# Windowed attention with sinks, then a gated feed-forward, on one core: k and q of seven tiles in packets of 4 tokens, tiles of the batches by turns, the first mask by TensorE, priorities by kind of work

## The chip, the cores and the metric

The kernel runs on one core of a Trainium2 chip. The metric is the device time of one execution in microseconds (us). The time of before is the median of three runs. Every duration of a single instruction comes from one further execution that the hardware profiler recorded.

## The reference

Inputs are q, k and v of shape (4, 8, 768, 64) in float32: 4 batches, 8 heads, 768 positions, head width 64. The number of sinks is 4 and the window is 128. Output is (3072, 512) in float32.

```python
scores = q @ k.T / sqrt(64)
keep = (key < 4) | ((0 <= query - key) & (query - key < 128))
a = softmax(where(keep, scores, -1e9))
x = (a @ v)                      # heads side by side: 3072 tokens x 512
xn = x / sqrt(mean(x*x) + 1e-6) * rms_g
g, val = xn @ w_gate, xn @ w_val # 512 x 1536 each
out = (g * sigmoid(g) * val) @ w_out   # 1536 x 512
```

## The kernel before

**Tiles and visits.** The 3072 tokens are 24 tiles of 128 tokens, six for each batch, taken batch after batch (`bt = b * NT + t`). A tile is attended to in two visits of four heads each, so there are 48 visits. A tile needs its own block of keys and the block before it in the same batch, and the four sink keys. The first block of a batch (`t == 0`) has only its own block.

**A tile's way in.** Three transfers issued by SyncE (SP) bring k, q and v of a tile as `[128 tokens, 8 heads, 64]` in float32 (`load`, L415): each run of memory is one head of one token, 256 bytes. `casts` (L317, L323) turns them into bf16. `qk_unit` transposes k and q, for the first 12 tiles by TensorE (L471) and a copy out of PSUM (L315, L317), later by a DMA transpose. The products with the sink keys are made there too (L491).

**A visit** (`visit`): score products into PSUM (L545). In a first block VectorE writes -1e30 over the forbidden half of the scores with a predicated copy (L558). In every other block it copies the older block's scores into the forbidden half (L567), so that one softmax row of 128 columns holds exactly the window, and copies the sink scores in (L578). Then a row maximum (L587), four exponents on ScalarE (L591), the exponent of the sinks (L597, L601), a transpose of the probabilities (TensorE for the first 12 visits, L609, then DMA, L618), two selections on GpSimd that split the current block from the older one (L625, L629), the products with v (L638, L646, L651), and a division by the row sum (L662, L665).

**After two visits** `rows` makes the normalisation (L675 to L685) and a transpose into `xnt` (L696, or DMA, L688).

**The feed-forward.** The first four tiles and the last two are groups of one tile, the others of two. `f_unit` makes one unit: gate products (L721), tanh on ScalarE (L735), value products (L721), two VectorE products (L739, L742) into `h`. A tile has three units, a pair of tiles six. `o_unit` makes the output product of a tile (L753), a copy (L764) and a store (L767). The weights come as nine transfers issued by GpSimd, which cast to bf16 on the way (L441, L447). `FIRST` gives their order and the earliest time of each in the plan; the first of them really waits until k of the second tile has landed (`HOLD`).

**The order of the work** is made by a planner. Every operation has engines with estimated times, what it reads and writes, and a rank. The planner plays the time forward and always picks the operation that can start first, and among equal starts the lowest rank. PSUM has one pair of banks for scores and six single banks (two singles also serve as a pair for the first 20 visits). The order that comes out is fixed on each engine. `ROOM` adds a margin, after 70 us of the plan, to the end of an operation of another engine that TensorE or VectorE waits for. `LEAD` lets visits run ahead of the feed-forward: visit n waits for feed-forward piece 2 * (n - LEAD). `fill` puts matmuls on a blank tile (L819) where the plan leaves TensorE free before 38 us.

Of the kernel before, what the change touches and what calls it, by code (L numbers as in the profile page):

```python
# [9 lines left out]
ALU = mybir.AluOpType  # L10
# [6 lines left out]
P = 128  # L17
NEG = -1.0e30
AHEAD = 2
LEAD = 12  # L20
NL = 3
# [6 lines left out]
FFRANK = 1000.0  # L28
QK_DMA = 12
FIRST = "g0:2 v0:10 g1:13 v1:18 g2:20 v2:27 o1:38 o2:39 o0:39"  # L30
SHARES = {"SP": 0.2, "POOL": 0.95}
ROOM = {"PE": 0.6, "DVE": 0.2}
ROOM_FROM = 70.0
# [4 lines left out]
SPLIT = 20  # L38
PACE = 7
# [19 lines left out]
class Plan:  # L59
# [10 lines left out]
    def op(self, alts, fn, reads=(), writes=(), rank=0.0, takes=None, banks=(), after=()):  # L70
        o = Op(alts, fn, rank)
# [18 lines left out]
    def dma(self, queue, issue, moves, fn, reads=(), writes=(), rank=0.0, lag=1.1, after=()):  # L90

        o = self.op([(queue, issue, issue)], fn, reads=reads, rank=rank, after=after)
        m = Op(queue, None, rank)
        m.moves, m.begin, m.left, m.lag = None, 0.0, moves, lag
        m.waits.add(o)
        for w in writes:
            if w in self.wrote:
                o.waits.add(self.wrote[w])
            o.waits.update(self.read.pop(w, ()))
            self.wrote[w] = m  # L100
        for r in reads:
            self.read[r].append(m)
        o.waits.discard(o)
        o.moves = m
        self.ops.append(m)
        return o

    def order(self):
# [59 lines left out]
        while len(done) < len(self.ops):  # L168
            pick = None
            for o in ready:  # L170
# [9 lines left out]
                key = (s, o.rank)  # L180
                if pick is None or key < pick[0]:
                    pick = (key, o, c, a)
            t = event()
            if t is not None and (pick is None or t <= pick[0][0]):
# [49 lines left out]
def kernel(  # L234
# [93 lines left out]
    KQT = ring("KQT", 2, [P, NT, 2, HP, P], BF16)  # L328
    KT = [x[:, :, 0] for x in KQT]
    QT = [x[:, :, 1] for x in KQT]  # L330
    KS = ring("KS", 2, [P, HP, 2, NS], BF16)
    VS = ring("VS", 2, [P, 2, 4 * VW], BF16)
# [8 lines left out]
    negbig = const.tile([P, 1], FP32, name="negbig")  # L341
    m_old = const.tile([P, P], I16, name="m_old")
    m_first = const.tile([P, P], I16, name="m_first")
# [33 lines left out]
    def c_masks():  # L377

        for m in (m_old, m_first):
            nc.gpsimd.memset(m, 1)  # L380
            nc.gpsimd.affine_select(
                out=m, in_=m, compare_op=ALU.is_gt, fill=0,
                base=0, pattern=[[1, P]], channel_multiplier=-1,
            )
        nc.gpsimd.memset(m_first[:, 0:NS], 0)

    def c_small():
        nc.vector.memset(negbig, NEG)
        nc.vector.memset(nhalf, -0.5)
        for i in range(2):  # L390
# [4 lines left out]
    def c_sinks():  # L395
        for i in range(2):
# [3 lines left out]

    plan.op(on(POOL=0.8), c_ident, writes=["ident"], rank=-3000)
    plan.op(on(DVE=0.6), c_small, writes=["small", ("KS", 0), ("KS", 1)] + [("V", i) for i in range(10)], rank=-3000)
    plan.op(on(ACT=1.4), lambda: nc.scalar.activation(out=warm, in_=nhalf, func=ACT.Exp), reads=["small"], rank=-3000)
    plan.op(on(POOL=1.4), c_masks, writes=["masks"], rank=-2999)
    plan.op(on(DVE=1.2), c_sinks, writes=[("VS", 0), ("VS", 1)] + [("PK", i) for i in range(NPS)], rank=-2999)

# [3 lines left out]
    def load(bt, rank):  # L410

        b, t = divmod(bt, NT)
        for i, src in enumerate((k, q, v)):
            n = (3 * bt + i) % len(ST)
            LOADED[bt, i] = plan.dma("SP", 0.45, 1.33, lambda src=src, n=n: nc.sync.dma_start(  # L415
                out=ST[n], in_=src[b, :, t * P:(t + 1) * P, :].rearrange("h t d -> t h d"),
            ), writes=[("ST", n)], rank=rank + 0.1 * i,
                after=VISIT[2 * bt - PACE:2 * bt - PACE + 1] if 2 * bt >= PACE else [])

    def casts(bt, rank):  # L420

        for i, nm in enumerate("kqv"):
            n = (3 * bt + i) % len(ST)
            if nm == "v":
                dst, key = V16[bt % len(V16)][:, :, 0:D], ("V", bt % len(V16))
            else:
                m = bt % len(SO)
                dst, key = SO[m][:, i].rearrange("p (h d) -> p h d", d=D), ("SO", m, i)
            if nm == "q":
                alts = on(DVE=0.4, ACT=on_act(DM))  # L430
                fn = lambda e, dst=dst, n=n: times(e, dst, ST[n], scale)
            else:
                alts = cast(DM) if bt < NT else on(POOL=0.13 + 0.84e-3 * DM)
                fn = lambda e, dst=dst, n=n: copy(e, dst, ST[n])
            plan.op(alts, fn, reads=[("ST", n)], writes=[key], rank=rank + 0.1 * i)

    def load_w(nm, i, rank):
# [3 lines left out]
        return plan.dma("POOL", 0.78, 3.1 if c1 - c0 > 256 else 1.8, lag=1.5, fn=lambda: nc.gpsimd.dma_start(  # L441
# [3 lines left out]
    def load_wo(part, rank):  # L445
        f0, f1 = 4 * part, 4 * part + 4
        return plan.dma("POOL", 0.78, 3.1, lag=1.5, fn=lambda: nc.gpsimd.dma_start(  # L447
# [5 lines left out]
    def qk_unit(b, t, rank):  # L453

        par = b % 2
        bt = b * NT + t
# [3 lines left out]
        if bt >= QK_DMA:  # L460
            plan.dma("SP", 1.2, 1.6, lambda: nc.sync.dma_start_transpose(
                out=KQT[par][:, t].rearrange("c a h p -> c (a h) p"), in_=SO[m].rearrange("p a d -> p (a d)")),
                reads=[("SO", m, 0), ("SO", m, 1)], writes=[("k", par, t), ("q", par, t)], rank=rank)
        else:
            for i, nm in enumerate("kq"):
                bk = Banks(ONES)

                def tr(i=i, bk=bk):
                    pt = bank(bk).bitcast(BF16)
                    for hp in range(HP):  # L470
                        nc.tensor.transpose(  # L471
                            out=pt[:, hp * P:(hp + 1) * P], in_=SO[m][:, i, hp * P:(hp + 1) * P], identity=ident,
                        )

                o = plan.op(on(PE=0.23), tr, reads=["ident", ("SO", m, i)], takes=bk, rank=rank + 0.1 * i, after=after)
                plan.op(evac(HP * P), lambda e, bk=bk, i=i: copy(
# [405 lines left out]
```

## Time and profile before

| | |
|---|---|
| median of three runs | 267.3 us (266.77 to 267.5) |
| the profiled execution's own time | 267.78 us |
| its span, first to last instruction | 266.0 us |
| granted TensorE clock | 0.999 |
| HBM read, written | 28.57 MB, 6.29 MB |
| transfers of k, q, v | 24 each of 256 KB, 4.6, 4.9, 5.1 us to landing (median) |
| weight transfers | 9 of 512 KB, medians of 9.2 to 10.6 us to landing |
| first gate product, first output product | at 19.56 us, at 55.86 us |

PE is TensorE's matmuls, PEld its loads of stationary weights, DVE is VectorE, ACT ScalarE, POOL GpSimd, SP SyncE. A group line gives line, engine, operation, output and input, count, then busy time and mean nanoseconds of one, then the engine's idle time before it and what ended that. In a chain line the numbers are start, duration and what. Matmuls overlap in a pipeline, so the durations of their records add up to more than the time that they hold the engine.

### The profile page before, as it was taken

What the parts mean: (1) busy time and instruction counts of PE and PEld (TensorE: products, weight loads), DVE (VectorE), ACT (ScalarE), POOL (GpSimd) and SP (SyncE); (2) the same over time, 40 slices, a digit from 0 to 9 for tenths busy, and PEclk for the clock granted to TensorE, in tenths of its full rate; (3) what the DMA queues carried; (4) which work ended last, traced back from release to release, by engine and by line L of the source; (5) the groups of instructions that cost most, each with busy time, mean ns of one, the idle gap of its engine ahead of it and who ended that gap; (6) DMA issues with size and microseconds to landing.
All of it is one profiled execution on the core that took longest, in us unless ns stands there. A gap on an engine that the chain in (4) does not pass through costs nothing.

```text
span 266.0 us, 7200 instructions
## 1 busy us (share of the span) xinstructions
PE 254.8 (96%) x2685; PEld 190.1 (71%) x2702; DVE 211.0 (79%) x510; ACT 147.3 (55%) x419; POOL 140.0 (53%) x272
## 2 busy tenths in 40 slices
PE   8998998999998999999999999999999999999994
PEld 6686877865666857858758668587587686785981
DVE  3977699999989898988959959679689599494641
ACT  2463676867767647456645467356664555551430
POOL 3566646579446897563637645734534446243100
PEclk9999999999999999999999999999999999999999
DMA  8999999979999989999999969969792431412311
GB/s 162 214 182 210 209 209 199 204 157 233 209 170 165 199 170 187 163 246 192 216 148 240 172 119 226 173 165 179 158 195 40 92 86 25 123 28 46 101 42 39
DMA packets 129155, 41.83 MB, mean 157 GB/s; under 512 B 121312, under 2 KB 125920, under 8 KB 129120
## 3 DMA queue, kind: packets, MB, share of 16 engines
q1 hardware_dynamic: 124368, 36.65, 75.2%
q0 software_dynamic: 4752, 4.72, 10.9%
q8 instruction: 21, 0.34, 0.6%
q14 instruction: 14, 0.11, 0.1%
HBM read 28.57 MB, written 6.29 MB: 131 GB/s over the span
## 4 chain that ended last, share of the span: by engine, by line
PE 81%; DVE 10%; DMA 5%; issue 2%; ACT 1%; POOL 0%; POOLq 0%
PE one L721 45%; PE one L753 22%; DMA wg_bf<-in_moe_w_gate_dram 5%; PE pair L545 4%; PE one L819 3%; DVE nmax L587 3%; PE one L646 2%; PE one L651 2%; PE one L638 1%; PE one L471 1%; DVE one L567 1%; PE one L609 1%; DVE h L742 1%; DVE so L323 1%; DVE x L665 1%
## 5 line engine op out<-in xcount | busy, mean ns | idle before, releaser
L721 PE MATMUL one<-xnt,wg_bf 128*128 128x256 bf16 (+1 forms) x720 | 72.0, 251 | 1.7 <-DMA wg_bf<-in_moe_w_gate_dram 1.0
L721 PE MATMUL one<-xnt,wv_bf 128*128 128x256 bf16 (+1 forms) x720 | 72.2, 251 | 0.3 <-DMA wv_bf<-in_moe_w_val_dram 0.2
L753 PE MATMUL one<-wo_bf,h 128*128 128x512 bf16 x271 | 68.1, 379 | 0.9
L735 ACT ACTIVATE th<-one 128x512 bf16<-128x512 f32 x72 | 42.7, 602 | 42.3 <-PE one L721 35.0
L721 PEld LDWEIGHTS <-wg_bf 128*128 128x128 bf16 x720 | 57.4, 98 | 10.5 <-issue 2.0
L721 PEld LDWEIGHTS <-wv_bf 128*128 128x128 bf16 x720 | 57.3, 98 | 9.7 <-issue 3.2
L739 DVE SCALAR_TENSOR_TENSOR p<-th,one 128x512 bf16<-128x512 bf16 x72 | 48.3, 677 | 15.1 <-ACT th L735 14.8
L591 ACT ACTIVATE ps<-pair,nmax 128x128 bf16<-128x128 f32 x152 | 43.7, 370 | 16.5 <-DVE nmax L587 8.6
L742 DVE TENSOR_TENSOR h<-p,one 128x512 bf16<-128x512 bf16 x72 | 48.3, 679 | 3.3 <-PE one L721 2.1
L753 PEld LDWEIGHTS <-h 128*128 128x128 bf16 x288 | 25.7, 98 | 26.3 <-issue 2.5
L683 POOL TENSOR_TENSOR xg<-x,grow 128x512 bf16<-128x512 bf16 x24 | 27.9, 1165 | 29.5 <-DVE x L665 27.1
L625 POOL TENSOR_SCALAR_AFFINE_SELECT cur<-pt 128x512 bf16<-128x512 bf16 x40 | 25.6, 639 | 29.5 <-DMA pt<-ps 21.5
L764 ACT ACTIVATE osb<-one 128x512 f32<-128x512 f32 x24 | 14.4, 599 | 24.0 <-PE one L753 23.8
L587 DVE TENSOR_REDUCE nmax<-pair 128x4 f32<-128x528 f32 (+1 forms) x38 | 26.5, 696 | 0.5
L567 DVE COPY_PREDICATED pair<-m_old,pair 128x512 f32<-128x512 int16 x32 | 22.0, 688 | 5.0 <-PE pair L545 4.0
L629 POOL TENSOR_SCALAR_AFFINE_SELECT old<-pt 128x512 bf16<-128x512 bf16 x40 | 25.8, 644 | 0.1
L597 POOL TENSOR_TENSOR sd<-sk,nmax 128x16 f32<-128x16 f32 x40 | 8.9, 224 | 25.7 <-DVE nmax L587 23.3
L665 DVE TENSOR_TENSOR x<-one,rden 128x256 bf16<-128x256 f32 x48 | 20.0, 417 | 0.5
L675 ACT ACTIVATE sq<-x 128x512 bf16<-128x512 bf16 x24 | 15.2, 634 | 9.2 <-DVE x L665 7.2
L819 PE MATMUL one<-blank 128*128 128x256 bf16 x132 | 19.2, 295 | 1.2 <-POOL blank L370 1.2
L662 DVE RECIPROCAL rden<-one 128x4 f32<-128x4 f32 x48 | 8.4, 176 | 10.8 <-PE one L651 9.4
L819 PEld LDWEIGHTS <-blank 128*128 128x128 bf16 x132 | 13.4, 106 | 3.8 <-POOL blank L370 1.2
(73 smaller groups left out, 305.2 us busy)
## 6 DMA issues: line engine op xcount, KB each, us to landing
st<-in_k_dram SPq DMA_DIRECT2D x24, 256.0 KB, 4.6
st<-in_q_dram SPq DMA_DIRECT2D x24, 256.0 KB, 4.9
st<-in_v_dram SPq DMA_DIRECT2D x24, 256.0 KB, 5.1
out_dram<-osb SPq DMA_DIRECT2D x24, 256.0 KB, 2.9
wg_bf<-in_moe_w_gate_dram POOLq DMA_DIRECT2D x3, 512.0 KB, 10.5
wv_bf<-in_moe_w_val_dram POOLq DMA_DIRECT2D x3, 512.0 KB, 9.2
wo_bf<-in_moe_w_out_dram POOLq DMA_DIRECT2D x3, 512.0 KB, 10.6
pt<-ps SPq DMA_TRANSPOSE x36, 3.3
```

What stands on the lines that cost most here:

```text
L567: nc.vector.copy_predicated(out=ap[:, :, P:2 * P], mask=m_old.unsqueeze(1).to_broadcast((P, hs.stop - hs.start, P)), data=ap[:, :, 0:P],)
L587: nc.vector.tensor_reduce(out=nm[:, hs], in_=ap[:, :, c0:2 * P], axis=AX.X, op=ALU.max, negate=True)
L591: plan.op(on(ACT=0.253), lambda h=h: nc.scalar.activation(out=PSM[r3][:, h, :], in_=head(h)[:, P:2 * P], func=ACT.Exp, bias=nm[:, h:h + 1] ...
L625: plan.op(on(POOL=0.6), lambda: nc.gpsimd.affine_select(out=cur, in_=PTT[r3][:, 0:4, :], compare_op=ALU.is_ge, fill=0.0, base=0, pattern=[ ...
L629: plan.op(on(POOL=0.6), lambda: nc.gpsimd.affine_select(out=old, in_=PTT[r3][:, 0:4, :], compare_op=ALU.is_gt, fill=0.0, base=0, pattern=[ ...
L683: plan.op(on(POOL=1.05), lambda: nc.gpsimd.tensor_tensor(out=xg, in0=X16[r], in1=grow, op=ALU.mult), reads=xs + ["g"], writes=[("XG", bt % ...
L721: nc.tensor.matmul(out=bank(bk)[:, i * n * P:(i + 1) * n * P].rearrange("p (t c) -> p t c", c=P), lhsT=w[:, kt, ft * P:(ft + 1) * P], rhs= ...
L735: plan.op(on(ACT=0.49), lambda: nc.scalar.activation(out=th, in_=b3(gb), func=ACT.Tanh, scale=0.5), banks=[gb], after=[o], writes=[("TH", ...
L739: plan.op(on(DVE=0.6), lambda: nc.vector.scalar_tensor_tensor(out=p1, in0=th, scalar=1.0, in1=b3(gb), op0=ALU.add, op1=ALU.mult,), banks=[ ...
L742: plan.op(on(DVE=0.6), lambda: nc.vector.tensor_tensor(out=HT[g % len(HT)][:, f0:f1, 0:n * P], in0=p1, in1=b3(vb), op=ALU.mult,), banks=[v ...
L753: nc.tensor.matmul(out=bank(bk)[:, 0:DM], lhsT=h[:, ft, tb * P:(tb + 1) * P], rhs=wo_bf[:, ft, :], start=(ft == 0), stop=(ft == FTN - 1),)
L819: done = plan.fill(done, lambda: nc.tensor.matmul(out=ONE[-1][:, 0:256], lhsT=blank[:, 0:P], rhs=blank, start=True, stop=True), 0.109)
```

## The change

1. **Packets.** k and q of the first seven tiles come with 4 tokens of one head in a packet (1 KB) and each in two transfers, one for every second head. Partitions then hold (head pair, group of four tokens), the casts reorder within the row, TensorE transposes as before, and the copy out of PSUM (`put`) writes with a stride of four to restore the order of tokens.
2. **Tiles by turns.** `bt = t * B + b`: the first four tiles are the first blocks of the four batches, then the second blocks, and so on. The k and q store keeps two blocks for each batch, used alternately, so "own" and "older" half of the scores swap places from block to block. Sink tables exist for all four batches.
3. **First mask.** In a first block TensorE writes the mask into PSUM (identity times a mask tile) and the score product is accumulated on it; VectorE's predicated copy goes.
4. **Plan.** Ranks are shifted by kind of operation, SP may take a lower rank within 0.4 us, and LEAD, the number of tiles in flight, the margins, the pace of the loads and the order and earliest times of the weights have new values.

```diff
-LEAD = 12
-NL = 3
+LEAD = 10
+NL = 4
+WIDE = 7
-FIRST = "g0:2 v0:10 g1:13 v1:18 g2:20 v2:27 o1:38 o2:39 o0:39"
+FIRST = "g0:10@2 g1:16@5 v1:15@6 v0:22@8 g2:19@0 v2:26@1 o0:33@7 o1:33@3 o2:30@4"
-ROOM = {"PE": 0.6, "DVE": 0.2}
-ROOM_FROM = 70.0
+ROOM = {"PE": 0.1, "DVE": 0.3, "ACT": 0.05, "POOL": 0.4, "SP": 0.05}
+WINDOW = {"SP": 0.4}
+WINDOW_TO = 100
+SHIFT = {"exp_sinks": 20, "load_2": 5, ... "square": 40, "greatest": -29.5, ... "exp": -1}
+EARLY = {"kq": 16, "av": -14.5, "m2": 16, ... "exp_sinks": -6.5}
+FEED = {"gate": 1000, "tanh": 6, "val": 10, "p1": 6, "h": 10, "out": 1000, "out_copy": 10, "store": 9}
+BEGIN = {(3, 2): 11, (5, 2): 36, (7, 0): 31, (8, 0): 38, (8, 1): 45, (9, 2): 79}
+ROOM_FROM = 50.0
+SOON = 6
+PACE0 = 9
...
+    def place(self, kind, rank):
+        if rank < -900:
+            return rank
+        if kind in FEED:
+            return (rank - FFRANK) / 2 + FEED[kind]
+        return rank + SHIFT.get(kind, 0.0) + (EARLY.get(kind, 0.0) if rank < 16 else 0.0)
...
+                until = s + (WINDOW.get(e, 0.0) if s < WINDOW_TO else 0.0)
+                for c in can:
+                    if c[3][0] == e and c[0][0] <= until and c[0][1] < pick[0][1] - 1e-9:
+                        pick = c
...
-    KQT = ring("KQT", 2, [P, NT, 2, HP, P], BF16)
+    KQT = ring("KQT", B, [P, 2, 2, HP, P], BF16)
...
-        b, t = divmod(bt, NT)
+        t, b = divmod(bt, B)
+        pace = PACE if bt >= SOON else PACE0
...
+            for half in (range(2) if bt < WIDE and i < 2 else (None,)):
+                wide = half is not None
+                LOADED[bt, i] = plan.dma(
+                    f"load_{i}", "SP", 0.45, 0.4 if wide else 1.2, ... nc.sync.dma_start(
+                        out=ST[n].rearrange("p (r j) d -> p r (j d)", r=2)[:, half] if wide else ST[n],
+                        in_=src[b].rearrange("(g r) t d -> r g t d", r=2)[half, :, t * P:(t + 1) * P].rearrange(
+                            "g (a j) d -> g a (j d)", j=4)
+                        if wide else src[b, :, t * P:(t + 1) * P, :].rearrange("h t d -> t h d"),
...
+                if bt < WIDE:
+                    dst, src = (x.rearrange(f"p ({y}) d -> p r j d", r=2) for x, y in ((dst, "j r"), (src, "r j")))
...
+                    if wide:
+                        copy(e, KQT[par][:, sl, i].rearrange("c g (a j) -> c j g a", j=4),
+                             pt.rearrange("c (j g a) -> c j g a", j=4, g=HP))
...
+        def m_mm():
+            for hs, ap in parts():
+                for i in range(0, hs.stop - hs.start, 2):
+                    nc.tensor.matmul(
+                        out=ap[:, i:i + 2, 0:P], lhsT=ident, rhs=m_first.unsqueeze(1).to_broadcast((P, 2, P)),
+                        start=True, stop=False, skip_group_check=True,
+                    )
+        if t == 0:
+            first = plan.op("mask_mm", on(PE=0.22), m_mm, takes=sb, reads=["ident", "first"], ...)
...
-        if t == 0:
-            def mask():
-                for hs, ap in parts():
-                    nc.vector.copy_predicated(
-                        out=ap[:, :, P:2 * P], mask=m_first.unsqueeze(1).to_broadcast((P, w, P)),
-                        data=negbig.unsqueeze(2).to_broadcast((P, w, P)),
-                    )
...
-    for b in range(B):
-        for t in range(NT):
-            bt = b * NT + t
+    for t in range(NT):
+        for b in range(B):
+            bt = t * B + b
             casts(bt, 2.0 * bt - AHEAD)
-            load_tile(bt + NL)
             qk_unit(b, t, 2.0 * bt - AHEAD)
...
+            load_tile(bt + NL)
             rows(bt, float(vn))
```

## The prediction

> **What bounds the kernel now.** I read the busy shares first, then the same table cut into stretches, then the DMA queues of the first 40 us, the chain of waits, and the cost groups of the lines that the change touches. From the page:
>
> ```profile
> PE 254.8 (96%) x2685; PEld 190.1 (71%) x2702; DVE 211.0 (79%) x510; ACT 147.3 (55%) x419; POOL 140.0 (53%) x272
> ...
> L819 PE MATMUL one<-blank 128*128 128x256 bf16 x132 | 19.2, 295 | 1.2 <-POOL blank L370 1.2
> ```
>
> TensorE (PE) looks full, but 132 of its matmuls are filler on a blank tile (L819). The stretches:
>
> ```profile
> 0.00:19.00 19.00, 17.18 (x162) 13.30 (x163) 12.88 (x53) 8.60 (x26) 9.54 (x29) 1.00 1.05 185
> 19.00:40.00 21.00, 19.07 (x288) 16.34 (x287) 16.57 (x45) 11.05 (x30) 12.42 (x21) 1.00 1.15 209
> 40.00:92.00 52.00, 49.25 (x634) 37.27 (x637) 49.98 (x136) 38.37 (x112) 34.50 (x67) 1.00 1.14 191
> 92.00:240.00 148.00, 147.42 (x1355) 107.10 (x1365) 121.04 (x261) 82.85 (x239) 80.42 (x152) 1.00 0.83 152
> ```
>
> The columns are span, busy PE, PEld, VectorE (DVE), ACT, POOL, clock, DMA share, GB/s. From 92 us PE is full (147.4 of 148) with DVE at 82%; from 40 to 92 DVE is full (50.0 of 52); before that DMA is (a share over 1: packets of two queues overlap in it).
>
> A busy matmul record includes pipeline time, so I count useful PE work by start-to-start distances in the timeline: 16 gate or value matmuls of 128 columns 0.95 us, 8 of 256 columns 0.87, 4 output matmuls 0.87, 4 transposes 0.22 (5: 0.28), scores of a visit 0.32 (first block of a batch 0.22), attention times value 0.35 (0.13), sink scores 0.11. With each stretch's own counts:
> - 0 to 19: 3.8 us of work, 15.2 lost.
> - 19 to 40: 13.8 of work (ten half units of the feed-forward make 9.5), 7.2 lost, 4.6 of it filler (42 x 0.109).
> - 40 to 92: 47.1 of work, 4.9 lost.
> - 92 to 240: 145.2, 2.8 lost; from 240 to the last output at 262.8: 22.8, nothing lost.
> So 232.7 us of work and 30.1 lost, 27.3 of it before 92 us, then 3.2 us of copy and store to the span's end, and 1.8 around the span: 267.8, the profiled run, 0.5 above the median of 267.3. The change can win only in those 27.3 us. The chain names what holds PE there:
>
> ```profile
> 7.90 0.75 DVE pair L558
> 8.66 0.77 DVE one L558 x2
> 9.43 0.59 DVE nmax L587
> ...
> 12.79 12.07 DMA wg_bf<-in_moe_w_gate_dram
> 24.90 1.07 PE one L721 x16
> 25.97 2.18 PE one L819 x20
> ```
>
> The first mask stands on DVE ahead of the first softmax; a gate weight is in flight for 12.1 us; and after its first unit PE spins on filler, because the second tile is not normalised before 30 us.
>
> **Packets.** In the first 40 us the queues show:
>
> ```profile
> q1 hardware_dynamic: 17712, 4.69, 61.0%
> q0 software_dynamic: 3168, 3.15, 48.6%
> ```
>
> 0.61 x 16 engines x 40 us / 17712 = 22 ns for a 256 B packet; weights (1 KB written) cost 0.486 x 640 / 3168 = 98 ns. After 244 us, stores with 2 KB packets and some short ones take 17.2% of 16 x 22 us: 60.5 us, less 608 x 22 ns, over 512 packets = 92 ns. No 1 KB load without cast exists. Its bounds are half a store packet, 46 ns, and a weight packet, 98 (a weight packet also reads twice its bytes, so the store is nearer). A straight line from 22 to 92 ns gives 52. A k or q tensor then costs 256 x 52 / 16 = 0.83 us of all engines against 1024 x 22 / 16 = 1.41: 0.58 saved, times 14 is 8.1 us (9.4 to -2.2 by the bounds), and nearly all 14 fall before 40 us. The Trainium skill (DMA: Bandwidth & Descriptors, Why small descriptors are slow) charges some 3 cycles of overhead on the 8 of a 256 B descriptor; an estimate from that, 35 cycles against 44, saves only 20%, 3.9 us, and my sum would gain 1.5 us less. The trace speaks against so small an overhead: 8 times the bytes cost 4.2 times as long, where the page's count gives 6.
>
> Two transfers instead of one are 14 more SP issues: 0.44 us unhindered (first load), 0.53 median (stores), so 6 to 7.4 us of SP's queue over some 45 us. Behind them on SP stand the next tiles' loads. Part of today's issue time is back-pressure (one issue held SP for 8.0 us), which fewer packets relieve; I take zero, keeping +1.5 us for a later second tile.
>
> **Tiles by turns, first mask on PE.** Eight visits of first blocks now come first. Each drops the DVE mask (six visits at 0.74, two at 2 x 0.48: 6.1 us in all) and stands where a later block's visit stood, with its predicated copy (0.69), sinks copy (0.17), two selections on POOL (0.64 each), a fifth transpose and the sinks' exponent. In the first 40 us DVE ran two masked first-block visits and six others: 2 x 0.8 + 6 x 0.86 = 6.8 us that go. Against this, the rearranged copies out of PSUM now write with a stride of four: 0.41 us today, bounds 0.41 and 0.68 (the two-operand DVE op on 512 elements), I take 0.60, near ACT's 0.585; half of 14 on DVE make +1.3, strided casts some +0.7, both 0 to 4.6 together. DVE is relieved by about 5 us, and two fewer lead visits (LEAD 12 to 10) move 2 x 2.16 us of visit work behind feed-forward. The Trainium skill (VectorE: DVE Perf Modes, What auto-detection actually checks) wants unit steps for the packed 16-bit mode, which speaks against this copy; today's 1.25 elements per ns agrees that the mode is on, and at 0.68 the sum would be 0.5 us higher.
>
> The later visits don't vanish: 40 of them remain, now denser after the start. That adds at most 4 x 0.12 us of DVE between 92 and 240, where it idles 27 us; their four extra POOL pairs (5 us) fit into its 67 idle. Eight mask products of two 256-column matmuls are new on PE: 16 x 0.109 = 1.7 us, zero if all fall into filler, 1.7 if none does; half do, +0.9. More memsets and a second batch pair of sink tables cost DVE under 1 us before the first k lands at 4 us: nothing.
>
> **The sum.** 0 to 19: two mask steps stand on the chain with 1.5 us; the first gate starts about that much earlier, since the weight is held only by the second tile's k: -1.5 (0 to -3). 19 to 40: the second tile's visits lose about 3 us of latency each and DVE stops queueing, but weights still come at some 3.2 us apiece (gate 1 let PE go at 24.9, value 1 at 28.1), and the first value block is now issued fifth: half of the 7.2 goes, -3.7 (-1 to -5.7). 40 to 92: DVE's relief and earlier output weights take 2.2 of 4.9 (0 to -4.4). Masks +0.9. The priorities, the planner's margin for work that crosses to PE (ROOM from 0.6 to 0.1) and the new begin times change no work; the cover is DVE's 18% idle after 92 us, taken at 0 (rival below). Together -6.5: 261.3 for a profiled run, 260.8 for the median. What is late next is weights: PE waits between 20 and 35 us for value weight 0 and gate weight 2.
>
> **Rivals.**
> - More is won (8%): lost time at its lower ends, -13.1, gives 254.2. For it: DMA and DVE are both relieved; against: weight traffic alone fills 19 us of all DMA engines.
> - The packets don't pay (12%): a 1 KB packet near 98 ns, or the doubled issues hold up tile two. Then 19 to 40 gives 1 and 40 to 92 gives 1: -1.5 -1 -1 +0.9 = -2.6, +1.5 for the issues at worst: 264.7 to 266.2. For it: cast weights at 98 ns; against: stores at 92 for twice the bytes. The Trainium skill (DMA: Bandwidth & Descriptors, Rules for kernel authors) says to coalesce small transfers; no run here shows a 128 KB load.
> - Slower (19%): PE stalls after 92 us. Its order is fixed; with 0.1 us of margin a matmul whose PSUM bank DVE releases late, or a score product behind it, blocks all that is queued. The price of one is in a busy stretch of today:
>
> ```profile
> 80.00:90.00 10.00, 8.93 (x109) 7.54 (x107) 9.32 (x26) 8.12 (x27) 7.18 (x13) 1.00 1.26 168
> ```
>
> 1.07 us idle in which 56 gate and value matmuls, 3.5 units, ran: 0.2 to 0.3 us a unit with DVE at 93%. Over 54 two-tile units 0.2 is 10.8 us: 271.6. It decides from 6.5 / 54 = 0.12 us per unit. Against it: the same table shows no such wait after 92 us.
> - No change (6%): the second rival with some 0.05 us a unit of the third.
>
> **The numbers.** The forecast has 55%, 256 to 264. About 0.3% (0.8 us) is what a measurement tells apart. Faster 0.55 + 0.08 + 0.12 = 0.75, same 0.06, slower 0.19. The range 255 to 269 leaves out the best few and the worse half of the slow case.
>
> **What would show it.** Right: filler matmuls between 19 and 40 us under 25; no DVE mask at the first visits; hardware packets in the first 40 us well under 17712 with DMA below full; first gate unit at 17 to 19 us, second tile's before 26; PE over 99% from 92 to 240. Wrong: PE below 97% there, or the first full unit later than today's 21.4 us with PE waiting on value weight 0.

## The result, and the profile after

The changed kernel takes 291.73 us (median of four runs, 291.33 to 293.7), the kernel before, on the same chip, 267.03 us: a ratio of 1.0943, 95% interval 1.0886 to 1.0999. The forecast was 260.8 us with a range to 269: wrong in sign and outside the range. Ratios, here and below, are to the kernel before on the same chip in the same session and leave out executions that ran in a slower state of the chip, so they can differ in the third digit from a quotient of the medians. The profiled execution took 291.64 us with a span of 289.6.

The page of after: busy shares, then the span in 40 slices of 7.24 us (busy tenths of TensorE, mean share of the 16 DMA engines).

```profile
PE 258.0 (89%) x2639; PEld 187.6 (65%) x2656; DVE 205.8 (71%) x492; ACT 157.4 (54%) x423; POOL 138.8 (48%) x272
...
PE   4773478975799999999999999999999999999994
...
DMA  2464789796999959999798999998999241440101
```

The 24.7 us are lost in front: TensorE is idle for 39% of the time until 50 us, and the DMA row, which is full there in the kernel before, starts at 2, 4, 6. The same stretches as before (span, busy PE, PEld, DVE, ACT, POOL, clock, DMA share, GB/s):

```profile
0.00:19.00 19.00, 11.03 (x63) 6.51 (x64) 6.63 (x34) 7.31 (x13) 5.38 (x23) 0.93 0.40 119
19.00:40.00 21.00, 10.37 (x94) 6.63 (x92) 9.28 (x26) 9.86 (x24) 6.50 (x12) 0.83 0.66 140
40.00:92.00 52.00, 44.41 (x602) 35.68 (x603) 38.65 (x100) 33.49 (x88) 26.93 (x54) 0.93 0.96 176
92.00:240.00 148.00, 146.75 (x1421) 104.99 (x1431) 123.20 (x279) 88.84 (x260) 88.93 (x166) 1.00 0.90 169
```

From 92 us TensorE is as full as forecast (146.75 of 148). Before that it lost 6 us of busy time in the first stretch against before, 9 in the second and 5 in the third. No engine takes their place: DVE is busy 9.28 of 21 us between 19 and 40, ACT 9.86, and DMA, which should have become the limit there, has a share of 0.66. The queues of the first 40 us (a digit is a tenth of 16 engines, in slices of 1 us; then packets, MB, share; the first line is of before, the others are of after):

```profile
DMA  0099999996999999999999999999999999977999
```

```profile
DMA  0022293222293355239589942222229449999447
...
q1 hardware_dynamic: 7650, 4.06, 34.7%
```

Most slices ahead of the first weight (issued at 18.17 us, before at 9.11) show a 2 or a 3, and those from 24 to 29 us, between weights, a 2: 20% to 30% of sixteen engines, and four of sixteen are 25%. The nines at 5 and 11 us follow the issues of the v tensors (3.33 and 9.62 us), which are walked token by token as before. While the DMA row shows 2 and 3, SP could not get its loads out. Its queue in after (start, duration, what, two halves of a tensor together); the last line is the second pair once the loads are mended, in spread16_unit below:

```profile
0.80 1.33 SPq L463 DMA_DIRECT2D st<-in_k_dram  x2
...
3.88 3.98 SPq L463 DMA_DIRECT2D st<-in_k_dram  x2
```

```profile
4.06 1.23 SPq L463 DMA_DIRECT2D st<-in_k_dram  x2
```

The first pair takes 1.33 us, the second 3.98 in place of 1.23: the queue is held back. (Issues of 8 us later on are no sign of the fault, since the kernel before has them too.) So k and q of the later tiles land late, and ACT shows what that does (its timeline; brackets are the idle time before, and what ended it):

```profile
7.77 1.29 ACT L352 COPY KQT<-one 128x512 bf16<-128x512 bf16 x1 [5.48 <-PE one L527]
...
15.77 0.63 ACT L358 ACTIVATE so<-st 128x512 bf16<-128x512 f32 x1 [4.09 <-DMA st<-in_q_dram]
...
23.05 0.63 ACT L358 ACTIVATE so<-st 128x512 bf16<-128x512 f32 x1 [2.04 <-DMA st<-in_q_dram]
...
32.21 0.63 ACT L358 ACTIVATE so<-st 128x512 bf16<-128x512 f32 x1 [5.45 <-DMA st<-in_q_dram]
35.54 0.62 ACT L352 CAST so<-st 128x512 bf16<-128x512 f32 x1 [2.70 <-DMA st<-in_k_dram]
```

ACT runs its list in order. The cast of a late q (L358) stands in that list ahead of exponents, squares and copies whose data is there. The chain of waits makes the loads the limit (start, duration, what):

```profile
15.65 7.31 DMA st<-in_q_dram
23.05 0.64 ACT so L358
23.73 0.41 PE one L527 x4
24.16 1.30 DVE KQT L354
...
25.96 9.50 DMA st<-in_k_dram
```

The first gate product starts at 43.5 us; before, at 19.6. Last, the copies that restore the order of tokens, in after and then the plain ones in before (count, then ns lowest/median/highest, then first and last start, up to 80 us):

```profile
L352 ACT COPY KQT<-one x11: 1268/1307/1392, 7.8 to 75.4; 128x512 bf16<-128x512 bf16 x11
...
L354 DVE COPY KQT<-one x3: 1281/1298/1299, 14.1 to 54.4; 128x512 bf16<-128x512 bf16 x3
```

```profile
L317 DVE COPY KQT<-one x14: 391/410/425, 5.6 to 80.0; 128x512 bf16<-128x512 bf16 x14
L315 ACT COPY KQT<-one x8: 579/586/587, 14.7 to 79.7; 128x512 bf16<-128x512 bf16 x8
```

The 14 copies of after take 1.31 us (ACT) and 1.30 us (DVE), against 0.586 and 0.410 us in the kernel before.

### The profile page after: what moved, and what is told of

Same layout as the page of the kernel before. It is cut to its first block, busy times and chain, and to the rows that moved or that the text cites. A ratio compares the mean times of both kernels' runs of the same rounds, so it can differ in the third digit from the quotient of the medians.

```text
span 289.6 us, 7148 instructions
## 1 busy us (share of the span) xinstructions
PE 258.0 (89%) x2639; PEld 187.6 (65%) x2656; DVE 205.8 (71%) x492; ACT 157.4 (54%) x423; POOL 138.8 (48%) x272
## 4 chain that ended last, share of the span: by engine, by line
PE 65%; DMA 19%; SPq 6%; ACT 3%; POOL 2%; issue 2%; DVE 2%; ACTq 0%; DVEq 0%; POOLq 0%
PE one L790 35%; PE one L822 18%; DMA st<-in_q_dram 13%; SPq L463 5%; DMA st<-in_k_dram 4%; PE pair L623 3%; PE one L715 2%; PE one L527 2%; DMA pt<-ps 1%; PE one L707 1%; PE one L720 1%; PE one L889 1%; SPq L845 1%; ACT KQT L352 1%; ACT so L358 1%
## 5 line engine op out<-in xcount | busy, mean ns | idle before, releaser
L790 PE MATMUL one<-xnt,wg_bf 128*128 128x256 bf16 (+1 forms) x720 | 72.8, 255 | 0.0
L822 PE MATMUL one<-wo_bf,h 128*128 128x512 bf16 x271 | 67.3, 379 | 1.1 <-issue 0.3
L790 PEld LDWEIGHTS <-wg_bf 128*128 128x128 bf16 x720 | 59.0, 100 | 8.2 <-issue 1.7
L660 ACT ACTIVATE ps<-pair,nmax 128x128 bf16<-128x128 f32 x156 | 45.5, 373 | 12.3 <-DVE nmax L656 6.1
L636 DVE COPY_PREDICATED pair<-m_old,pair 128x512 f32<-128x512 int16 x35 | 24.2, 692 | 13.6 <-PE pair L623 7.9
L656 DVE TENSOR_REDUCE nmax<-pair 128x4 f32<-128x528 f32 (+1 forms) x39 | 27.3, 700 | 0.9 <-PE pair L623 0.4
L527 PE MATMUL one<-ident,so 128*128 128x128 bf16 x96 | 10.4, 245 | 17.7 <-ACT so L358 8.7
L833 ACT ACTIVATE osb<-one 128x512 f32<-128x512 f32 x24 | 14.4, 603 | 18.7 <-PE one L822 18.6
L358 ACT ACTIVATE so<-st 128x512 bf16<-128x512 f32 x15 | 9.5, 636 | 26.7 <-DMA st<-in_q_dram 26.7
L527 PEld LDWEIGHTS <-so 128*128 128x128 bf16 x96 | 7.1, 109 | 21.4 <-ACT so L358 9.4
L352 ACT COPY KQT<-one 128x512 bf16<-128x512 bf16 x15 | 16.5, 1114 | 7.2 <-PE one L527 7.1
L744 ACT ACTIVATE sq<-x 128x512 bf16<-128x512 bf16 x24 | 15.2, 632 | 9.3 <-DVE x L734 9.1
```

Of the source, the lines that this page charges most:

```text
L527: nc.tensor.transpose(out=pt[:, x * P:(x + 1) * P], in_=SO[m][:, i, x * P:(x + 1) * P], identity=ident,)
L636: nc.vector.copy_predicated(out=ap[:, :, own], mask=m_old.unsqueeze(1).to_broadcast((P, hs.stop - hs.start, P)), data=ap[:, :, other],)
L656: nc.vector.tensor_reduce(out=nm[:, hs], in_=ap[:, :, seen], axis=AX.X, op=ALU.max, negate=True)
L660: plan.op("exp", on(ACT=0.253), lambda h=h: nc.scalar.activation(out=PSM[r3][:, h, :], in_=head(h)[:, own], func=ACT.Exp, bias=nm[:, h:h + ...
L790: nc.tensor.matmul(out=bank(bk)[:, i * n * P:(i + 1) * n * P].rearrange("p (t c) -> p t c", c=P), lhsT=w[:, kt, ft * P:(ft + 1) * P], rhs= ...
L822: nc.tensor.matmul(out=bank(bk)[:, 0:DM], lhsT=h[:, ft, tb * P:(tb + 1) * P], rhs=wo_bf[:, ft, :], start=(ft == 0), stop=(ft == FTN - 1),)
```

## Experiments

**Theory A**: a wide load is confined to four DMA engines. The memory side of the transfer is walked as `g a (j d)`: outermost are four heads, then 32 groups of tokens, then the packet. The DMA row fits four engines at work. The Trainium skill (DMA: Bandwidth & Descriptors, "Why a DMA increments its semaphore by 16 and not by 1") says that a transfer is given the largest number of engines, up to 16, that divides the slowest dimension of both of its sides, and its "Rules for kernel authors" say that an outermost dimension below 16 confines the whole transfer to at most that many. By that, 128 partitions on one side and 4 heads on the other give 4, and the trace agrees: a share of 0.2 to 0.3 in the slices with wide loads alone. The prediction used that page's section on small descriptors, and not this rule. Two counts from the traces say four without any rule. A wide load of after raises its semaphore in 5 steps, the first of them before its data moves (for the first load at 1.90 us, its first packet starts at 2.26, the other four steps come from 4.37 to 4.92); each v load of after, and each load of spread16 below, takes 16 steps. And between 24 and 29.5 us, with almost nothing but wide loads under way, 4.5 packet records are open at a time in the mean and never fewer than four; in spread16 it is 18.7 in the same stretch, where weights run as well (records of two queues overlap). The rivals: the strided copies cost the time, or the new order with its priorities does.

I compare experiments by ratio, one point being 2.7 us.

**spread16: the same packets, with 32 outermost.** The partition order becomes (group, head pair), so the copy out of PSUM reads accordingly, and still writes with a stride of four.

```diff
-    "g (a j) d -> g a (j d)", j=4)
+    "g (a j) d -> a g (j d)", j=4)
...
-    pt.rearrange("c (j g a) -> c j g a", j=4, g=HP))
+    pt.rearrange("c (j a g) -> c j g a", j=4, g=HP))
```

> The 28 transfers of 1 KB packets are the same in number and size, but the memory side is walked with its dimension of 32 outermost instead of its dimension of 4; the copy out of PSUM reads in the new order and still writes with a stride of four. Theory A (the wide transfers run on a quarter of the DMA engines, as the DMA share of 0.2 in the first microseconds says, and the late k and q starve TensorE): the DMA share of the first loads rises from 0.2 to 0.9, the first k lands near 4 us instead of 6.6, no wide transfer takes over 8 us, and of the 24 us lost some 16 to 20 come back: 272 to 276 us. Theory B (the copies out of PSUM at 1.3 us are the main loss): no more than 5 us come back, 287 us or more. Theory C (the new order and the priorities are the loss): 285 us or more even with early loads.

Measured: 271.66 us, ratio 1.0120 (1.0082 to 1.0157). Its first 40 us of DMA, and its stretches:

```profile
DMA  0056799889989988999999999999999999999999
```

```profile
0.00:19.00 19.00, 15.23 (x139) 9.96 (x140) 12.99 (x53) 12.04 (x25) 9.34 (x30) 1.00 0.81 200
19.00:40.00 21.00, 14.62 (x187) 11.52 (x186) 14.62 (x42) 16.86 (x44) 11.65 (x23) 0.84 1.16 228
```

The order of instructions on every engine is that of after, a packet of a wide load has the same median of 46 ns, and the copies still take 1.30 us. What differs is the order in which a transfer walks its source, with the reading side of the copies, and 8.2 of the 9.4 points come back (1.0943 to 1.0120). The twos are fives to nines, the first gate product starts at 30.0 us in place of 43.5. Theory A holds. But this is still slower than before, so more is wrong.

**unit_write: the copy writes in order and reads with a stride instead.** Loads as in after.

```diff
-    copy(e, KQT[par][:, sl, i].rearrange("c g (a j) -> c j g a", j=4),
-         pt.rearrange("c (j g a) -> c j g a", j=4, g=HP))
+    copy(e, KQT[par][:, sl, i].rearrange("c g (a j) -> c g a j", j=4),
+         pt.rearrange("c (j g a) -> c g a j", j=4, g=HP))
```

> Only the copy of the transposed k and q out of PSUM changes: it writes with unit stride and reads with a stride. Theory A (quarter of the DMA engines): the copies fall from 1.3 us to 0.4 to 0.6, and as the loads stay late the time falls by 1 to 4 us, 288 to 291. Theory B (the copies): 14 copies by 0.7 to 0.9 us on a path that TensorE waits for give 10 us back, near 281. If the read with a stride costs as much as the write, the copies stay at 1.3 us and the time at 291.

Measured: 292.57 us, ratio 1.0919 (1.0887 to 1.0952): no different from after. The copies themselves:

```profile
L352 ACT COPY KQT<-one x11: 563/586/599, 7.8 to 75.3; 128x512 bf16<-128x512 bf16 x11
...
L354 DVE COPY KQT<-one x3: 690/691/691, 14.1 to 53.7; 128x512 bf16<-128x512 bf16 x3
```

ACT's went from 1.307 to 0.586 us, DVE's from 1.298 to 0.691, and nothing came of it, where 1 to 4 us had been expected even under theory A: behind the late loads their time is covered.

**narrow: 256-byte packets, all else as in after** (the planner makes its order anew).

```diff
-WIDE = 7
+WIDE = 0
```

> No tile is wide: all k and q come in packets of 256 B, one transfer each, with plain copies out of PSUM; tiles by turns, first mask and priorities stay, and the planner works out its order anew. Theories A and B together (the packets' edit is the whole loss): 258 to 266 us, below before, as the other parts were forecast to gain. Theory C (order, priorities, margins): 280 us or more. Between them both have a share.

Measured: 283.58 us, ratio 1.0567 (1.0537 to 1.0598), where I had expected less than before. The last stretch:

```profile
92.00:240.00 148.00, 138.39 (x1258) 96.63 (x1265) 109.83 (x242) 78.75 (x233) 76.61 (x144) 0.99 0.76 144
```

TensorE now loses 9.6 us after 92 us, where after loses 1.3; its longest waits there are for the transpose of the normalised rows (2.1 us) and for exponents on ACT (1.2). By the expectation, 280 or more was the sign that the new order and its priorities are the loss. But the single edit changed the estimated times, and the planner drew another order than that of after; spread16, which keeps the order of after, is 4.5 points faster. My reading is that the ranks and begin times of the change do not suit the redrawn order. So this run says little on the packets: it is an experiment with two edits, one of them hidden.

**spread16_unit: both mends together**, the load of spread16 and the copy of unit_write (reading `"c (j a g) -> c g a j"`).

> Both edits: the dimension of 32 outermost, and the copy out of PSUM with unit write stride. Theories A and B together: 256 to 262 us, below before and 2 to 5 us below the kernel with narrow packets, since the 1 KB packets were seen at 46 ns. Theory C: still 280 or more.

Measured: 269.04 us, ratio 1.0023 (0.9990 to 1.0056): as fast as before, where 256 to 262 us had been expected. With the loads spread, the copies are worth 1.0 point (2.6 us). ACT's timeline shows what is left (the last line is of before):

```profile
21.92 0.63 ACT L358 ACTIVATE so<-st 128x512 bf16<-128x512 f32 x1 [5.15 <-DMA st<-in_q_dram]
22.63 0.62 ACT L352 CAST so<-st 128x512 bf16<-128x512 f32 x1
23.15 0.62 ACT L744 ACTIVATE sq<-x 128x512 bf16<-128x512 bf16 x1
```

```profile
15.81 0.63 ACT L675 ACTIVATE sq<-x 128x512 bf16<-128x512 bf16 x1
```

ACT stands for 5.15 us before the cast of the fourth tile's q (by the semaphore that it waits for; the expectations below call it the fifth tile's), and the first square (L744), without which no feed-forward can start, is queued behind it and behind the cast of the fifth tile's k: 23.15 us, against 15.81 before. The first eight pairs of half transfers hold SP's queue for 1.2 to 1.3 us each, a whole v tensor for 0.60. Three theories for this: **D**, loads land later than the plan expects because they are issued twice, and a fixed order makes everything behind their casts wait; **E**, the margins and ranks put the square at a wrong place; **F**, the tiles by turns need more loads at the start than DMA can bring.

**one_transfer, issue_true, square0: three edits to the plan**, each on spread16_unit. One transfer and one plan operation per wide tensor; a price of 0.63 us in place of 0.45 for an issue of SP; no shift of rank for squares.

```diff
-            for half in (range(2) if bt < WIDE and i < 2 else (None,)):
+            wide = bt < WIDE and i < 2
...
-                        "g (a j) d -> a g (j d)", j=4)
+                    "r g (a j) d -> a g r (j d)", j=4)
```

```diff
-                    f"load_{i}", "SP", 0.45, 0.4 if wide else 1.2, ...
+                    f"load_{i}", "SP", 0.63, 0.4 if wide else 1.2, ...
```

```diff
-    "exp_sinks": 20, "load_2": 5, "xnt": 3.5, "recip": -1, "square": 40, "greatest": -29.5, ...
+    "exp_sinks": 20, "load_2": 5, "xnt": 3.5, "recip": -1, "greatest": -29.5, ...
```

> As spread16_unit, but k and q of a wide tile come in one transfer each (256 KB, 1 KB packets) instead of two. Open is why spread16_unit stands at 269.0 and not at the forecast 260.8. Theory D (loads later than the plan believes: the pair of issues takes SP 1.25 us where the plan counts 0.9, so ScalarE, whose order is fixed, waits 5.15 us for the q of a later tile before it does the first tile's square, and the first gate product comes at 28.9 us instead of 19.6): one issue of some 0.6 us brings the fifth tile's q 4 to 5 us earlier, the first gate product to 22 to 25 us, and the time to 263 to 266. Theory E (margins and ranks cost it throughout) or F (tiles by turns cost it): 267 to 270.

> As spread16_unit, with the plan told 0.63 us for each SP issue of a load instead of 0.45; the chip's work is the same, only the order is made anew. Theory D: the plan no longer puts casts of tiles that have not landed ahead of the first tile's square; the wait of ScalarE for q falls below 2 us and the time to 262 to 267. Theories E and F: 267 to 272.

> As spread16_unit, without the shift of 40 in the rank of the squares (the first step of the normalisation on ScalarE). Theory D in its strong form (the late square is put behind casts by its rank): the first square runs at 16 to 18 us, the first gate product at 20 to 24, and the time is 262 to 266. If the planner places the square there by its time and not by its rank, the order hardly changes and the time stays at 267 to 270.

Measured, as ratios: one_transfer 1.0333 (1.0282 to 1.0383), issue_true 1.0367 (1.0295 to 1.0439), square0 1.0275 (1.0226 to 1.0325). All three are slower than spread16_unit, and alike, where theory D had 262 to 267 us and its rivals at most 272: the planner draws another order each time, and that order stalls late. The last stretch of one_transfer:

```profile
92.00:240.00 148.00, 139.33 (x1270) 98.08 (x1269) 109.99 (x239) 79.46 (x236) 73.83 (x140) 0.98 0.71 145
```

139.33 of 148 us, against 146.17 in spread16_unit; issue_true has 140.48, square0 143.37. In front one_transfer was better than spread16_unit (PE 18.80 of 21 us between 19 and 40, against 15.91): its first square is at 16.9 us and its first gate product at 23.6, as D had it. In square0 they are at 22.3 and 31.8, so the square's rank alone did not put it late. By their totals these three tell nothing of D, E or F; with narrow they suggest that the ranks and begin times fit one drawn order, but which of them no run shows.

**turns_mask: only the tiles by turns and the mask on TensorE.** 256-byte packets in one transfer, ranks, margins, pace and weights' times as before.

> Tiles by turns and the first mask on TensorE alone: narrow packets, and the ranks, margins, LEAD, number of tiles in flight, weights' order and times as in the kernel before. The forecast gave these two parts most of VectorE's relief, worth some 3 to 4 us: 263 to 265. Theory F (the order by turns costs time by itself): 268 or more. Theory E (the new ranks and margins are what makes the kernel with narrow packets 283.6): 263 to 268, far below 283.6.

Measured: 292.45 us, ratio 1.0921 (1.0865 to 1.0977), where I had expected a gain. The first gate product starts at 18.4 us, earlier than before. Then (chain, and the third stretch):

```profile
11.09 7.68 DMA wv_bf<-in_moe_w_val_dram
18.77 13.91 DMA st<-in_v_dram
32.69 14.44 DMA st<-in_k_dram
```

```profile
40.00:92.00 52.00, 40.45 (x528) 29.84 (x526) 41.24 (x115) 33.19 (x98) 29.62 (x57) 0.90 0.91 162
```

From the start of its issue to its landing a v tensor takes 13.9 us and a k tensor 14.4 us, after a value weight that had gone ahead of them. The casts of those tensors stand on DVE, which waits 9.1 us for k and 5.8 for q until 60 us, and TensorE drops to 40.45 of 52. It is the same mechanism as in after, from another cause: here all DMA engines are full (share 1.18 between 19 and 40) and the weights take their turn, in after four of the engines are. So the turns and the mask do not pay by themselves in the order that the planner drew for them, and F holds in that form; no run parts the turns from that drawn order.

**before_wide: only the packets**, over 16 engines, one transfer, copies with ordered writes, in the order of before on every engine.

```diff
+                out=ST[n].rearrange("p (r j) d -> p r (j d)", r=2),
+                in_=src[b].rearrange("(g r) t d -> r g t d", r=2)[:, :, t * P:(t + 1) * P].rearrange(
+                    "r g (a j) d -> a g r (j d)", j=4),
```

> The kernel before, its plan and its order untouched, with k and q of the first seven tiles in 1 KB packets, one transfer each, the dimension of 32 outermost, and copies out of PSUM with unit write stride. If the packets are worth what the forecast said (some 8 us of all DMA engines), loads and weights land earlier in the first 40 us and the fixed order uses it: 262 to 265.5. If DMA was not what the first 40 us waited for, or the order can't use earlier data: 266.5 to 268. The copies cost 0.1 us more each on VectorE, under 1 us in all.

Measured: 270.08 us, ratio 1.0071 (1.0046 to 1.0097): slightly slower, and above both of the ranges that had been expected. The hardware queue of the first 40 us, and the third stretch:

```profile
q1 hardware_dynamic: 10210, 5.51, 54.4%
```

```profile
40.00:92.00 52.00, 48.55 (x629) 36.22 (x627) 50.04 (x137) 38.43 (x115) 33.07 (x64) 1.00 1.03 177
```

The packets do what they should (17712 packets and 61.0% before), and TensorE gets nothing. In the order of before, the first gate waits for a weight, not for a tile (20.4 us, before 19.6). And DVE, already the full engine between 40 and 92 us, carries the longer copies: a mean of 565 ns in place of 410 over 14 copies, 2.2 us. That this makes the 2.0 us is likely from the size, but no run parts it from the rest. What the walk with four outermost costs in the order of before is not known: the run for it (before_wide4) gave no result.

**before_mask: only the mask on TensorE**, in the kernel before (order drawn anew).

```diff
+                        out=ap[:, i:i + 2, P:2 * P], lhsT=ident, rhs=m_first.unsqueeze(1).to_broadcast((P, 2, P)),
+                        start=True, stop=False, skip_group_check=True,
...
-                    nc.vector.copy_predicated(
-                        out=ap[:, :, P:2 * P], mask=m_first.unsqueeze(1).to_broadcast((P, w, P)),
```

> The kernel before with the first mask by TensorE alone; the planner orders anew. The forecast gave 1.5 us on the first chain and under 1 us of cost on TensorE: 265 to 267. If each new order of the plan is a draw of several us (as the three kernels at 275 to 278 suggest), it lies anywhere from 264 to 275 and TensorE's waits differ after 92 us.

Measured: 270.03 us, ratio 1.0075 (1.0047 to 1.0103).

```profile
40.00:92.00 52.00, 47.65 (x625) 36.29 (x622) 48.57 (x134) 38.30 (x118) 37.04 (x75) 1.00 1.11 189
```

The first gate product starts at 17.2 us in place of 19.6, and 1.6 us of TensorE is lost again between 40 and 92 (47.65 against 49.25), with DVE 1.4 us less busy there. An earlier start is not an earlier end.

**same_order_one: D, with the order held.** The order of instructions on every engine is that of spread16_unit; the plan still counts two issues for a tensor, but only one is made, and it brings all of it.

```diff
-    lambda ...: nc.sync.dma_start(
-        out=ST[n].rearrange("p (r j) d -> p r (j d)", r=2)[:, half] if wide else ST[n],
+    lambda ...: None if half == 0 else nc.sync.dma_start(
+        out=ST[n].rearrange("p (r j) d -> p r (j d)", r=2) if wide else ST[n],
...
-            "g (a j) d -> a g (j d)", j=4)
+            "r g (a j) d -> a g r (j d)", j=4)
```

> spread16_unit with exactly its order on every engine; where a wide tensor came in two transfers, the first one's place issues nothing and the second one's place brings the whole. Theory D (loads later than the plan believes, so that ScalarE waits 5.15 us for a q ahead of the first square): SP gets to the fifth tile's q some 4 us earlier, that wait falls below 2 us, and the time to 263 to 266. If SP's issues are not what makes these loads late: 267 to 270.

Measured: 264.27 us (263.38 to 265.1), ratio 0.9858 (0.9824 to 0.9893): faster than both kernels, 1.65 points (4.4 us) better than spread16_unit. The same place on ACT, and the stretches:

```profile
16.02 0.68 ACT L358 ACTIVATE so<-st 128x512 bf16<-128x512 f32 x1
16.54 0.67 ACT L352 CAST so<-st 128x512 bf16<-128x512 f32 x1
17.05 0.69 ACT L744 ACTIVATE sq<-x 128x512 bf16<-128x512 bf16 x1
```

```profile
0.00:19.00 19.00, 15.50 (x151) 10.59 (x152) 13.39 (x56) 12.35 (x34) 10.44 (x32) 1.00 0.89 231
19.00:40.00 21.00, 17.50 (x274) 14.81 (x273) 17.47 (x49) 15.52 (x45) 16.28 (x29) 1.00 1.20 225
40.00:92.00 52.00, 52.00 (x644) 38.66 (x642) 45.59 (x114) 34.47 (x100) 32.90 (x64) 1.00 1.09 194
92.00:240.00 148.00, 147.19 (x1374) 105.15 (x1371) 120.13 (x264) 82.30 (x238) 80.12 (x149) 1.00 0.78 146
```

The 5.15 us wait is gone: the cast of that q starts at 16.02 us in place of 21.92, the square at 17.05 in place of 23.15, the first gate at 22.7 in place of 28.9. TensorE is full from 40 us on. Theory D holds, and E is not needed for these 4.4 us, since ranks and margins are the same. SP's queue is only part of how. The issue of that q, in spread16_unit and here:

```profile
12.58 1.25 SPq L463 DMA_DIRECT2D st<-in_q_dram  x2
```

```profile
10.37 0.61 SPq L463 DMA_DIRECT2D st<-in_q_dram  x1
```

SP is done with it 2.85 us earlier, but it lands 6.6 us earlier (15.26 in place of 21.83): it is also 3.7 us less in flight. In spread16_unit the first weight is issued at 12.07 us, ahead of that q, here at 12.54, behind it. What that does is seen within spread16, on the two halves of the same q: the first is issued at 12.34 us, ahead of the weight (12.67), and lands after 3.3 us, the second at 12.99, behind it, and lands after 6.4. So a later issue can cost more by falling behind a weight than by its own lateness. How much of the 4.4 us that makes stays open, since no run moves the weight alone.

**same_order_256: the same order again, with the packets back at 256 bytes**, plain casts and plain copies.

```diff
-        in_=src[b].rearrange("(g r) t d -> r g t d", r=2)[:, :, t * P:(t + 1) * P].rearrange(
-            "r g (a j) d -> a g r (j d)", j=4)
+        in_=src[b, :, t * P:(t + 1) * P, :].rearrange("h t d -> t h d"),
...
-    copy(e, KQT[par][:, sl, i].rearrange("c g (a j) -> c g a j", j=4),
-         pt.rearrange("c (j a g) -> c g a j", j=4, g=HP))
+    copy(e, KQT[par][:, sl, i].rearrange("c h p -> c (h p)"), pt)
```

> The order of every engine is that of same_order_one (264.27 us, ratio 0.9858 to before); only the packets of k and q of seven tiles go back to 256 bytes (one transfer of 256 KB per tensor, plain casts and plain copies out of PSUM). Packets pay: by 22 ns against 46 ns for four times the bytes, 14 tensors cost 14 x (1024 x 22 - 256 x 46) / 16 = 9.4 us more of all DMA engines; with DMA full from 4 to 40 us half of that or more reaches TensorE: 268 to 274 us, TensorE below 16.5 us busy between 19 and 40. Packets don't pay (as they did not in the order of before, ratio 1.0071): 262.5 to 265.5, since the shorter plain copies (DVE 0.41 for 0.51 us) and casts give back what later landings take.

Measured: ratio 0.9981 (0.9939 to 1.0024), so 1.2 points (3.3 us) are the packets' in this order, net of the plain copies and casts that come with the smaller ones.

```profile
0.00:19.00 19.00, 14.13 (x120) 8.77 (x120) 9.12 (x43) 9.64 (x25) 7.38 (x28) 1.00 1.01 196
19.00:40.00 21.00, 17.87 (x247) 14.49 (x248) 19.23 (x57) 16.19 (x47) 16.12 (x28) 0.92 1.14 201
```

The first gate is at 27.5 us in place of 22.7. The total is where the theory that packets pay put it; its sign, TensorE below 16.5 us between 19 and 40, did not come (17.87): more of the loss is ahead of 19 us (14.13 against 15.50). The same q is late again: its issue at 12.23 us is behind the first weight's (11.54), it lands at 20.59 us, and ACT is idle for 3.79 us before its cast. So the packets that cost 0.7 points in the order of before earn 1.2 here, where the first gate product waits behind that cast and not for a weight.

## Why the prediction was wrong

**The step that failed** is in the part on packets: "A k or q tensor then costs 256 x 52 / 16 = 0.83 us of all engines". The 52 ns was good: the packet records of the wide loads have a median of 46 ns. The 16 was never argued. It came from today's loads, where a mean over 16 engines is right. With 4 the same line reads 256 x 46 / 4 = 2.9 us of the engines in use, against 1.41 before; for 14 tensors that is 21 us more where I had booked 8.1 us less. spread16 gave back 8.2 points, 22 us. The first is time of DMA engines and the second time of the kernel, so that they come out alike is partly luck. The one rival on packets ("don't pay") had a price for the packet and one for the issue, and none for the number of engines.

**The strided copy** was taken at 0.60 us with 0.41 and 0.68 as bounds. It took 1.30 on both engines, outside them. The bounds came from slower row kinds of DVE, none of which writes 16-bit elements with a stride. With a strided read the DVE copy takes 0.691 us, near my 0.68; a strided write takes 0.61 us more on DVE, and 0.72 us more than a plain copy on ACT. The rule that I cited from the Trainium skill (VectorE: DVE Perf Modes, "What auto-detection actually checks"), unit steps for the packed 16-bit mode, had the direction right; it gives no price for the write, and none for ACT. In after this was hidden; with the loads mended it was 2.6 us, where I had about 0.5 at the upper bound.

**The doubled issues on SP** were taken at zero with 1.5 us kept for a late second tile. I had nearly their size (6 to 7.4 us of SP's queue; a pair took 1.25 us, a whole tensor 0.60, so 14 x 0.65 = 9.1) and what stands behind them. They cost 4.4 us. The miss is in the step "Part of today's issue time is back-pressure (one issue held SP for 8.0 us), which fewer packets relieve; I take zero": in spread16_unit each of the first issues still holds SP for 0.6 us, and the fourth tile's q was 6 us late to ACT.

**The slower rival** had the wrong place. I put the risk of a fixed order after 92 us, in the small margins. There after is full (146.75 of 148). The engines that run in order stood at the front instead, behind casts of tensors that had not landed. The prediction named the next tiles' loads as what is queued behind an added issue, but not what is queued behind their casts: "a load lands late, and all that stands behind its cast waits" was no rival in it.

**Two slips in its sums** are too small to matter: 6 x 0.74 and 4 x 0.48 us of masks make 6.4 us, not 6.1, and half of 7.2 is 3.6, not 3.7.

**What held.** No DVE mask at first visits, and 16 mask products. Fewer hardware packets in the first 40 us (7650 under 17712), but for the wrong reason, as the share showed at once: 0.40 in the first stretch beside idle engines is not relief, it is confinement. The signs for under 25 filler matmuls between 19 and 40 us (22) and for PE over 99% after 92 us (99.2%) came as well, though the forecast was wrong. Only the late first gate product told, and it waited for tiles, not for value weight 0 as that sign had it. The turns with the mask, the mask alone and the packets alone each lose (1.0921, 1.0075, 1.0071), where their sum was booked as a gain. Put together with the new plan, and mended, they give 1.4%, where the sum had said 2.4%. Nor does the gain come where the sum had it. In same_order_one, 40 to 92 us is full (52.00 against 49.25: 2.75 us, forecast 2.2), but the first gate is at 22.7 us, not 17 to 19, and until 40 us 139 gate and value matmuls run, against 160 before.

**What stays open**: why the changed ranks stall so readily when the order is drawn anew, and which of them; of the ranks only the square's was varied alone. How much of the 4.4 us is SP's queue and how much the weight that the fourth tile's q falls behind. And whether before_wide's 2.0 us are DVE's copies.

## What to carry to other kernels

Price a transfer by the engines that it uses as well as by its packets: look at the outermost dimension on both sides (here 32 in place of 4 on the memory side was worth 22 us), and where the DMA share lies near a simple fraction while engines wait for loads, look at the walk of the access pattern before anything else. In a fixed order, the cast of a tensor that lands late blocks everything behind it on its engine, so ask for each added transfer what is queued behind its first reader, and which large transfer the later issues now fall behind. And when a planner redraws the order for each edit, test an edit with the order held: here the same edit, one transfer in place of two, gave +3.1 points with a new order and -1.65 with the order held.

## What the runs showed of the hardware that was not expected

- A load in one kernel took 4 of 16 DMA engines or all, by the order of two dimensions in its source: a share of 0.2 to 0.3 or of 0.5 to 0.9 while tiles were loaded, 5 or 16 steps of its semaphore, and 22 us of the kernel.
- Two halves of one tensor, issued 0.65 us apart in spread16 with the issue of a 512 KB weight between them, landed after 3.3 and 6.4 us.
- A copy of 128x512 bf16 out of PSUM: 0.410 us on DVE and 0.586 on ACT in order; 0.691 and 0.586 with a strided read; 1.298 and 1.307 with a write of stride four. ACT does not mind the strided read, and both mind the write.
- The granted clock fell to 0.83 between 19 and 40 us in after, where TensorE was busy half of the time (0.84 in spread16), while in the kernel before, with filler, it was 1.00. The records of the mask products into the pair of banks have a median of 328 ns in after and 273 in same_order_one.
